# Attention: K and Q loaded in the row order of memory, by two transfers each

## The chip, the cores and the metric

The kernel runs on one core of a Trainium2 chip. The metric is the device time of one execution in microseconds, the median of the runs shown.

## The reference

The program is an attention with a compressive memory, followed by a layer of routed experts. For each of 8 x 8 heads, q, k and v have 576 rows of 64 float32 numbers:

```python
scores = (1/8) * q @ k.T, causal mask        # 576 x 576 per head
local  = softmax(scores) @ v
q_p    = where(q > 0, q, exp(q) - 1) + 1
mem    = (q_p @ M_prev) / (q_p @ z_prev + 1e-6)
x      = g * mem + (1 - g) * local           # g = sigmoid(beta), per head
# x as 4608 rows of 512; each row goes to one of 8 experts, 576 rows to each,
# in the order of the gate's logits; out = relu(x @ w1[e]) @ w2[e]
```

The change concerns the attention alone.

## The kernel before

**Units.** `attention` (line 290 on) works through 16 units `u` of 4 heads each: unit 2b holds heads 0 to 3 of batch b, unit 2b+1 heads 4 to 7. Several units are in work at once. A head's 576 rows are 4 blocks of 128 rows and a rest of 64.

**Layout.** `kf` and `qf` hold K and Q of a unit as 128 partitions x 18 blocks x 64 numbers. Blocks 4h to 4h+3 are the full blocks of head h. Blocks 16 and 17 hold the rests: heads 0 and 1 share block 16 (upper and lower 64 partitions), heads 2 and 3 share block 17. `load` (365) therefore needs for each of K and Q one transfer per head (373, 128 KB) and two for the rests (380, 32 KB each): six per unit. V has a similar layout, and a separate tile `vF` for head 3 of each unit (371, 372, 378).

**From K and Q to scores.** `turned` (443) splits the float32 numbers into two float16 halves in `h16` (the higher by ScalarE or GpSimd, the lower as a difference at line 457), turns the 18 blocks on TensorE (466) and copies them to `kT` and `qT`. SyncE copies 64 partitions of `kT` to `kB` (471) and of `qT` to `qM` (475); ScalarE or VectorE may do it instead. `maxes` (478) forms scores once to find the maximum of each row, with VectorE's reductions (480, 481). The 18 x 128 maxima are turned, read out into `mr` and sent by SyncE into a row of `qM` (540). `scores` (571) forms the scores a second time with the maxima subtracted, ScalarE takes the exponential, and `outs` (631) multiplies with V and with the memory. The result of a unit, `xs`, is written head by head; GpSimd does the last step of a head (`nsub`, 697).

**The end of a unit.** `fin` (699) has SyncE turn `xs` into `xT` by a DMA transpose (step `xt_`, 703) and write `xs` to memory (716, 717). TensorE multiplies `xT` by the gate's weights (step `lg`, 724).

**What sets the order.** Every step is an entry of one list `SC`, with the steps it depends on, the engine or engines that may do it, and the buffers that it takes and gives back. `PR_ORDER` (36) is a written list: the sequence of all 3118 step numbers, the chosen engine for each step with a choice, and the buffer for each step that takes one. `SC.run(PR_ORDER)` (766) issues the steps in that sequence, and each engine works through its own in order. SyncE does nothing but start transfers: all loads, `kB<-kT`, `qM<-qT`, the maxima, `xt_` and the writes of `xs` stand in its one queue. The expert part (`moe_all`) has its own plan.

**The first unit** is cut finer: `uo['0']` lists the pieces in which it is split, turned and copied, blocks 8 to 18 (heads 2 and 3 and the rests) first.

Of the kernel before, what the change touches and what calls it, by code (L numbers as in the profile page):

```python
# [33 lines left out]
 'uo': {'0': {'hord': [2, 3, 0, 1], 'ls': 1.0, 'mg': [[1], [0]], 'pc': [[8, 18], [0, 8]], 'pc_l': [[8, 18], [0, 8]], 'pc_p': [[8, 13], [13, 18], [0, 4], [4, 8]], 'pc_t': [[8, 18], [0, 8]], 'px': 2.0},  # L34
        'L': {'pet': 1}}}
PR_ORDER = ('''
# [253 lines left out]
def attention(ctx,tc,q,k,v,M_prev,z_prev,beta,wg,xd,L1,NB,cst,rcst):  # L290
# [60 lines left out]
    def K(t,i,a=0,b=18):  # L351

        return [(t,i,x) for x in range(a,min(b,16))]+([(t,i,16),(t,i,17)] if b==18 else [])
# [4 lines left out]
    def hord(u): return UO(u).get('hord') or [0,1,2,3]  # L358
# [3 lines left out]
    for u in range(NU):  # L362
        for h in FH(u): vfi[u,h]=len(vfi)
    def LS(u): return UO(u).get('ls',0.0)
    def load(u,nm,src,off,roff):
        b,hf=divmod(u,2); t={'k':kf,'q':qf,'v':vf}[nm][u%2]
        for j,h in enumerate(hord(u)):
            s=src[b,4*hf+h,off:off+512,:].rearrange('(t p) d -> p t d',p=128)
            if nm=='v' and h in FH(u):
# [66 lines left out]
    for u in range(NU):  # L436
# [125 lines left out]
        def vpieces(pc):  # L562
            return [(a,NVT if b_==18 else min(b_,NVT)) for a,b_ in pc]
# [7 lines left out]
        def scores(u=u,U2=U2,U3=U3):  # L571
# [25 lines left out]
            for j,h in enumerate(hord(u)):  # L597
                if len(gs)==2 and j%2==0: sj4(gs[j//2])
                B_=[]
                for w in range(3):  # L600
                    def f(x,h=h,w=w):
# [8 lines left out]
                        else:  # L610
                            two(p[:,0:256],4*h+2,qs(2)); mk(p[:,0:128])
                            for y in (2,0,1,3): two(p[:,256+64*y:320+64*y],4*h+y,lambda t: t[:,16+h2,64*hh:64*hh+64],last=True)
# [579 lines left out]
```

## Time and profile before

| | |
|---|---|
| median of 3 runs | 902.94 us (897.38 to 905.11) |
| profiled execution | 900.57 us, its span 898.5 us |
| TensorE (PE) busy | 809.4 us, 90% |
| VectorE (DVE), ScalarE (ACT), GpSimd (POOL) busy | 638.4, 584.2, 561.0 us |
| mean granted TensorE clock | 0.953 |
| DMA | 231675 packets, 120.58 MB |

Times in the rows are microseconds from the first instruction of the span, unless marked ns. L457 is line 457 of the kernel before. SPq is SyncE's queue of transfers; a row of it is the time that SyncE takes to start the transfer, not the transfer itself. The granted clock is a share of full speed: 1.0 is 2.4 GHz, 0.5 is 1.2 GHz. In a timeline, the bracket at the end says how long the engine had been idle before and what ended that. "x3" in a merged row is three instructions.

### The profile page before, as it was taken

Reading aid. Unit: us, or ns where it says so; the run is one execution under the profiler, and the core shown is the slowest. Engines: PE = TensorE matmul, PEld = TensorE weight load, DVE = VectorE, ACT = ScalarE, POOL = GpSimd, SP = SyncE. Lnnn points to the kernel's source line nnn. Section 1 sums busy time; section 2 is a strip of 40 time slices with the busy share of each in tenths; the row PEclk is TensorE's granted clock in tenths of the full one; section 3 lists DMA queues with packets and bytes.
Section 4 is the critical chain, followed back from the end, with each engine's and each line's share of the span. In section 5 each row is a group of like instructions: output and inputs, shape, how many; then the busy total and the mean of one; then the engine's idle time right before and its main releaser. Section 6 shows DMA issues by size and latency. Waiting matters only on the chain.

```text
span 898.5 us, 24664 instructions
## 1 busy us (share of the span) xinstructions
PE 809.4 (90%) x9432; PEld 539.1 (60%) x9432; DVE 638.4 (71%) x2276; ACT 584.2 (65%) x1062; POOL 561.0 (62%) x599
## 2 busy tenths in 40 slices
PE   4988989899999999997138999999999999999995
PEld 2767878787888888887016445454444444444442
DVE  8988969788898899887897778787868774111020
ACT  5988969686999889873337575757383845562110
POOL 4988869797899898885024383838183737852101
PEclk9999979899999999999557999999999999999998
DMA  5566687676666747433042565655564738920001
GB/s 126 128 139 148 156 168 147 158 156 134 147 148 158 171 99 163 99 73 84 1 140 102 187 141 211 139 215 130 204 141 142 200 127 190 279 109 18 36 12 42
DMA packets 231675, 120.58 MB, mean 134 GB/s; under 512 B 199493, under 2 KB 208709, under 8 KB 231557
## 3 DMA queue, kind: packets, MB, share of 16 engines
q1 hardware_dynamic: 225669, 100.13, 45.6%
q0 software_dynamic: 5888, 18.88, 6.8%
q8 instruction: 74, 1.21, 0.5%
q14 instruction: 44, 0.36, 0.1%
HBM read 72.40 MB, written 18.87 MB: 102 GB/s over the span
## 4 chain that ended last, share of the span: by engine, by line
PE 62%; issue 10%; DVE 10%; DMA 6%; POOL 5%; SPq 4%; ACT 2%; another core or an unknown queue 0%; POOLq 0%; DVEq 0%; ACTq 0%
PE py L834 16%; PE ph L834 15%; PE pb L306 13%; PE avo L306 9%; PE pb L466 3%; DVE scr L1075 2%; DMA qM<-qT 2%; PE prem L834 2%; SPq L373 2%; POOL h L457 2%; PE avm L306 1%; DMA xT<-xs 1%; PE pr L834 1%; DMA qf<-in_q_dram 1%; SPq L380 1%
## 5 line engine op out<-in xcount | busy, mean ns | idle before, releaser
L991 POOL TENSOR_TENSOR wl<-wst,wh 128x1024 f16<-128x1024 f32 x62 | 131.4, 2142 | 82.2 <-ACT wh L990 75.3
L834 PE MATMUL ph<-xT,wh 128*128 128x512 f16 (+1 forms) x560 | 164.8, 368 | 2.9 <-DVE hl L1034 1.4
L1053 POOL DMA_INDIRECT out_dram<-ys,idx x40 | 39.0, 975 | 118.7 <-ACT ys L1048 99.4
L834 PEld LDWEIGHTS <-wh 128*128 128x128 f16 x1072 | 69.2, 99 | 60.4 <-issue 4.7
L306 PE MATMUL pb<-qT,kT 128*128 128x64 f16 (+3 forms) x576 | 104.4, 243 | 1.0 <-ACT pf L627 1.0
L306 PE MATMUL pb<-qM,kB 128*128 128x64 f16 (+3 forms) x576 | 97.7, 242 | 5.7 <-DMA qM<-mr 3.8
L1034 DVE SCALAR_TENSOR_TENSOR hl<-ph,hh 128x512 f16<-128x512 f32 x64 | 44.0, 688 | 80.3 <-ACT hh L1033 77.5
L480 DVE TENSOR_REDUCE mx<-pb 128x1 f32<-128x512 f32 (+3 forms) x192 | 89.4, 503 | 14.6 <-PE pb L306 14.1
L834 PE MATMUL ph<-xT,wl 128*128 128x512 f16 (+1 forms) x280 | 98.4, 366 | 0.0
L834 PE MATMUL py<-wh,hh 128*128 128x512 f16 x256 | 97.0, 379 | 1.2 <-ACT hh L1033 0.8
L834 PE MATMUL py<-wl,hh 128*128 128x512 f16 x256 | 97.0, 379 | 0.0
L620 ACT ACTIVATE ph<-pb 128x512 f16<-128x512 f32 x144 | 85.2, 601 | 17.6 <-PE pb L306 11.4
L834 PE MATMUL prem<-xT,wh 128*128 128x64 f16 x512 | 96.6, 193 | 0.0
L1033 ACT ACTIVATE hh<-ph 128x512 f16<-128x512 f32 x64 | 38.0, 593 | 76.5 <-PE ph L834 55.4
L1075 DVE TENSOR_SCALAR_CACHE_REDUCE scr<-p_LwT,th 128x320 f16<-128x320 f32 x168 | 85.1, 543 | 2.9 <-DVE th L1082 0.2
L306 PE MATMUL pb<-kT,qM 128*128 128x512 f16 (+5 forms) x384 | 82.5, 312 | 5.1 <-DMA qM<-qT 2.4
L1073 ACT ACTIVATE scs<-p_LwT,th 128x320 f16<-128x320 f32 x84 | 47.0, 560 | 58.4 <-DVE th L1082 45.0
L834 PEld LDWEIGHTS <-hh 128*128 128x128 f16 x512 | 47.3, 97 | 55.8 <-ACT hh L1033 1.0
L306 PE MATMUL avo<-V,ph 128*128 128x65 f16 x1344 | 76.7, 193 | 0.0
L306 PE MATMUL avo<-V,pl 128*128 128x65 f16 x672 | 73.4, 196 | 1.3 <-POOL pl L628 1.3
L913 POOL DMA_INDIRECT xg<-xd,idx x40 | 38.9, 973 | 53.7 <-DVE sa L934 36.8
L306 PEld LDWEIGHTS <-ph 128*128 128x128 f16 x1344 | 69.2, 98 | 4.8 <-issue 1.5
(304 smaller groups left out, 2415.7 us busy)
## 6 DMA issues: line engine op xcount, KB each, us to landing
wst<-in_moe_w_dram SPq DMA_DIRECT2D x32, 1024.0 KB, 8.0
kf<-in_k_dram SPq DMA_DIRECT2D x64, 128.0 KB, 2.9
qf<-in_q_dram SPq DMA_DIRECT2D x64, 128.0 KB, 3.2
xd<-xs SPq DMA_DIRECT2D x16, 512.0 KB, 4.3
vf<-in_v_dram SPq DMA_DIRECT2D x48, 128.0 KB, 2.8
qM<-qT SPq DMA_DIRECT2D x15, 288.0 KB, 3.6
kB<-kT SPq DMA_DIRECT2D x14, 288.0 KB, 3.3
vF<-in_v_dram SPq DMA_DIRECT2D x16, 128.0 KB, 2.7
```

The costliest lines, as they stand in the source:

```text
L306: def MM(*a,**kw): mm(*a,skip_group_check=True,**kw)
L466: for i in range(a,b_): nc.tensor.transpose(p[:,128*(i-a):128*(i-a)+128],g()[:,i],cst['idh'])
L480: R=lambda o,i: nc.vector.tensor_reduce(o,i,axis=mybir.AxisListType.X,op=ALU.max)
L620: c=SC.add('Eh',[('A',486)],lambda x,a=a: nc.scalar.activation(phs_[x.buf['ph']][:,0:512],pbb[a.buf['pb']],AF.Exp,scale=0.125),acq=('ph',) ...
L834: def MM(*a,**kw): mm(*a,skip_group_check=True,**kw)
L913: SC.add('gather',[('P',1250 if i<4 else 1200,'p',0,(1250,'n'))],lambda x: G_.indirect_dma_start(out=xg[0:r_,i],out_offset=None,in_=xd,in_ ...
L991: SC.add('sp',[('P',2079)],lambda x,ws=ws,k=k,s=s: G_.tensor_sub(wl[:,k,s],ws(),wh[:,k,s]),r=[key+('h',)],w=[key+('l',)],after=[b],rel=rel ...
L1033: b=SC.add('hh',[('A',478)],lambda x,a0=a0,f=f: A_.activation(hh[:,f],phb[a0.buf['ph']],AF.Relu),w=[('hh',f)],after=[y],prio=pr('hh',n,pos ...
L1034: SC.add('hl',[('V',602)],lambda x,a0=a0,f=f: V_.scalar_tensor_tensor(hl[:,f],phb[a0.buf['ph']],0.0,hh[:,f],op0=ALU.max,op1=ALU.subtract), ...
L1053: SC.add('scat',[('P',1250 if i<4 else 1200,'p',0,(1250,'n'))],lambda x,e=e,i=i,r_=r_: G_.indirect_dma_start(out=outv[5*n+i],out_offset=ba ...
L1073: SC.add('sign',[('A',547)],lambda x,j=j,t_=t_,c_=c_: A_.activation(scs[j-KV],LwT,AF.Sign,bias=t_[:,4:5],accum_out=c_[:,j:j+1]),r=['LwT',( ...
L1075: V(462,lambda x,j=j,t_=t_,c_=c_: V_.tensor_scalar(scr[j],LwT,t_[:,j+1:j+2],0.0,op0=ALU.is_ge,op1=ALU.add,accum_out=c_[:,j:j+1]),r=['LwT', ...
```

## The change

K and Q of a unit are loaded as 2304 rows in the order of memory, 18 blocks of 128 rows: two transfers of 9 blocks each, four for each of K and Q in the first unit. Turned, the heads stand side by side: head h takes columns 576h to 576h+575 of `kT`, `qT`, `kB` and `pT` (the turned q_p). A head now begins and ends within a block, so the keys of dependence (`KC`, `KH`, `KR`) are counted by columns. `qM` keeps the old order, because the maxima's row does; the copy from `qT` becomes two, of 512 and of 64 columns of each head. V is loaded as before. The first unit is split at block 9 instead of 8. The number of steps falls from 3118 to 3013, and `PR_ORDER` is a new list throughout, with new choices of engine and buffer.

```diff
- 'uo': {'0': {'hord': [2, 3, 0, 1], 'ls': 1.0, 'mg': [[1], [0]], 'pc': [[8, 18], [0, 8]], ...
+ 'uo': {'0': {'hord': [2, 3, 0, 1],
...
+              'pc': [[9, 18], [0, 9]],
+              'pc_d': [[9, 13], [13, 18], [0, 4], [4, 9]],
...
 PR_ORDER = ('''
-5 21 2 23 26 4 22 25 0 24 1 28 27 3 32 31 41 30 43 42 29 45 6 44 47 248 ...
+5 21 2 22 24 1 23 26 4 25 3 27 28 37 6 39 240 0 41 38 241 43 42 34 40 44 ...
...
+    def KC(t,i,a,b): return K(t,i,a//128,(b+127)//128)
+    def KH(t,i,h): return KC(t,i,576*h,576*h+576)
+    def KR(t,i,h2): return KC(t,i,1152*h2+512,1152*h2+576)+KC(t,i,1152*h2+1088,1152*h2+1152)
...
     def load(u,nm,src,off,roff):
         b,hf=divmod(u,2); t={'k':kf,'q':qf,'v':vf}[nm][u%2]
+        if nm!='v':
+            rows=src[b,4*hf:4*hf+4].rearrange('h s d -> (h s) d')
+            for j,(a,b_) in enumerate(UO(u).get('pc_d') or [[0,9],[9,18]]):
+                SC.add('l'+nm,dq(182*(b_-a),hw=530),lambda x,a=a,b_=b_: nc.sync.dma_start(out=t[:,a:b_],in_=rows[128*a:128*b_].rearrange('(t p) d -> p t d',p=128)),w=K(nm+'f',u%2,a,b_),prio=pr('l'+nm,u,j*LS(u)))
+            return
...
-            SC.add('l'+nm,dq(182,hw=640),lambda x,hh=hh: nc.sync.dma_start(out=t[64*hh:64*hh+64,16:18,:],in_=r[hh,roff:roff+64,2*hf:2*hf+2,:]),w=[(nm+'f',u%2,16+hh)],prio=pr('l'+nm,u,1.5*LS(u)))
...
-        for a,b_ in MVP(u):
-            SC.add('qmove',... nc.sync.dma_start(out=qM[u%3][0:64,a:b_],in_=qTs[U3][64:128,a:b_]) ...
+        for h0,nh,kd in ([(0,4,0),(0,4,1)] if u else [(2,1,0),(3,1,0),(2,2,1),(0,1,0),(1,1,0),(0,2,1)]):
+            w_=512 if kd==0 else 64; o_=512*h0 if kd==0 else 2048+64*h0; n=nh*w_
+            def mv(x,h0=h0,nh=nh,kd=kd,w_=w_,o_=o_,n=n,U3=U3,u=u):
+                o=fl(qM[u%3])[0:64,o_:o_+n].rearrange('p (h k) -> p h k',k=w_); i=fl(qTs[U3])[64:128].rearrange('p (h k) -> p h k',k=576)[:,h0:h0+nh,512*kd:512*kd+w_]
+                if x.var=='d': nc.sync.dma_start(out=o,in_=i)
+                else: cp(x.var,o,i)
...
-            kq=lambda h,n: kT[:,4*h:4*h+n,:].rearrange('p a k -> p (a k)')
+            kq=lambda h,n: kT[:,576*h:576*h+128*n]
...
-            for c0_ in range(a,b_,8):
+            for c0_,c1_ in [(c,min(c+8,b_)) for c in range(a,b_,8)] if b_-a!=9 else [(a,a+4),(a+4,b_)]:
...
-            def two(o,jb,qsl,rows=None,last=False):
-                l=kT[:,jb] if rows is None else kT[:,jb,rows]
+            def two(o,h,jb,a,b,last=False):
+                l=slice(576*h+128*jb,576*h+min(128*jb+128,576)); qs=slice(576*h+a,576*h+b)
+                MM(o,kT[:,l],qT[:,qs],start=True,stop=False)
+                MM(o,kb_[:,l],qm_[:,512*h+a:512*h+b] if a<512 else qm_[:,2048+64*h:2112+64*h],start=False,stop=last)
...
-                        l=pT[:,4*h+i] if i<4 else pTf[:,128*(16+h2)+64*hh:128*(16+h2)+64*hh+128]
+                        l=pTf[:,576*h+128*i:576*h+128*i+128]
```

## Rows read from the trace of the kernel before

**Rows 1.** Windows by stage: length, busy us of PE, PEld, DVE, ACT, POOL, PEclk, DMA, GB/s.

```profile
0.00:22.00 22.00, 9.96 (x63) 6.12 (x64) 19.19 (x50) 12.91 (x21) 10.14 (x63) 1.00 0.56 126
22.00:73.00 51.00, 45.89 (x709) 37.08 (x706) 45.50 (x125) 45.65 (x87) 45.06 (x50) 1.00 0.59 133
73.00:221.00 148.00, 135.63 (x2285) 115.91 (x2282) 120.24 (x354) 117.39 (x223) 120.54 (x154) 0.93 0.74 156
221.00:395.00 174.00, 171.21 (x3036) 147.43 (x3034) 157.45 (x453) 155.12 (x292) 156.31 (x168) 1.00 0.58 130
...
424.00:898.50 474.50, 420.30 (x2831) 208.44 (x2829) 274.96 (x1233) 237.59 (x412) 210.20 (x143) 0.93 0.45 132
```

**Rows 2.** Waits of TensorE, 22 to 424 us: total us, times, longest.

```profile
PE pb L306 <- DMA xT<-xs: 6.6, 2, 3.6
PE pb L306 <- DMA qM<-mr: 3.8, 2, 2.1
PE pb L306 <- DMA qM<-qT: 2.4, 4, 1.0
PE pb L306 <- DMA qM<-zr: 1.9, 1, 1.9
```

**Rows 3.** Timeline of GpSimd and ScalarE: start, length, line, out<-in, idle before.

```profile
101.68 0.80 POOL L697 TENSOR_TENSOR xs<-xt,xs 128x320 f16<-128x320 f32 x1 [0.45 <-ACT xs L347]
...
204.09 0.25 ACT L347 CAST mr<-pb 18x128 f16<-18x128 f32 x1
```

**Rows 4.** Timeline of the transfers that SyncE starts (SPq).

```profile
102.43 2.83 SPq L373 DMA_DIRECT2D kf<-in_k_dram  x3
...
108.92 1.08 SPq L373 DMA_DIRECT2D qf<-in_q_dram  x2
...
110.63 3.80 SPq L703 DMA_TRANSPOSE xT<-xs  x1
...
210.04 0.84 SPq L540 DMA_DIRECT2D qM<-mr  x1
```

**Rows 5.** Timeline of TensorE, behind its two longest waits after the start.

```profile
117.29 0.70 PE L306 MATMUL pb<-wgs,xT 128*128 128x16 f16 x20 [3.59 <-DMA xT<-xs]
...
165.89 0.69 PE L306 MATMUL pb<-wgs,xT 128*128 128x16 f16 x20 [2.97 <-DMA xT<-xs]
```

**Rows 6.** Windows behind three waits of TensorE (clock third from the end).

```profile
115.00:130.00 15.00, 12.71 (x147) 11.23 (x148) 7.47 (x21) 7.02 (x13) 7.18 (x9) 0.66 0.77 169
165.00:175.00 10.00, 9.11 (x93) 7.42 (x94) 5.70 (x18) 5.82 (x13) 6.27 (x8) 0.66 0.74 186
210.00:220.00 10.00, 7.97 (x149) 7.37 (x149) 5.95 (x25) 5.36 (x10) 3.99 (x6) 0.83 0.94 166
```

**Rows 7.** Tiles kf, qf, qM: starts, ns min/median/max, first and last start.

```profile
L373 SPq DMA_DIRECT2D kf<-in_k_dram x64: 367/537/1807, 0.7 to 291.7; - x64
L380 SPq DMA_DIRECT2D kf<-in_k_dram x32: 596/628/1072, 1.8 to 293.5; - x32
...
L373 SPq DMA_DIRECT2D qf<-in_q_dram x64: 367/514/1828, 4.5 to 342.0; - x64
L380 SPq DMA_DIRECT2D qf<-in_q_dram x32: 595/623/1581, 5.6 to 334.0; - x32
...
L475 SPq DMA_DIRECT2D qM<-qT x15: 507/547/964, 29.6 to 361.7; - x15
```

**Rows 8.** Page, DMA issues: count, KB each, median us to landing.

```profile
kf<-in_k_dram SPq DMA_DIRECT2D x64, 128.0 KB, 2.9
...
qM<-qT SPq DMA_DIRECT2D x15, 288.0 KB, 3.6
```

**Rows 9.** Timeline of the start: SyncE's transfers, ScalarE.

```profile
0.74 1.01 SPq L373 DMA_DIRECT2D kf<-in_k_dram  x2
...
3.23 0.62 SPq L380 DMA_DIRECT2D kf<-in_k_dram  x1
...
6.47 1.28 ACT L347 ACT_TABLE_LOAD   x1 [6.47 <-DMA kf<-in_k_dram]
```

More of the change, by code (lines that the diff above doesn't have):

```diff
@@ L33 @@
  'strict': 1,
- 'uo': {'0': {'hord': [2, 3, 0, 1], 'ls': 1.0, 'mg': [[1], [0]], 'pc': [[8, 18], [0, 8]], 'pc_l': [[8, 18], [0, 8]], 'pc_p': [[8, 13], [13, 18], [0, 4], [4, 8]], 'pc_t': [[8, 18], [0, 8]], 'px': 2.0},
+ 'uo': {'0': {'hord': [2, 3, 0, 1],
+              'ls': 1.0,
+              'mg': [[1], [0]],
+              'pc': [[9, 18], [0, 9]],
+              'pc_d': [[9, 13], [13, 18], [0, 4], [4, 9]],
+              'pc_l': [[9, 18], [0, 9]],
+              'pc_p': [[9, 13], [13, 18], [0, 4], [4, 9]],
+              'pc_t': [[9, 18], [0, 9]],
+              'px': 2.0},
         'L': {'pet': 1}}}
 PR_ORDER = ('''
[75 rows of a table removed]
[72 rows of a table added]
 ''','''
[2 rows of a table removed]
[2 rows of a table added]
 ''','''
[6 rows of a table removed]
[6 rows of a table added]
 ''')
@@ L351, in K, with BK @@
     def K(t,i,a=0,b=18):
-        return [(t,i,x) for x in range(a,min(b,16))]+([(t,i,16),(t,i,17)] if b==18 else [])
+        return [(t,i,x) for x in range(a,b)]
+    def KC(t,i,a,b): return K(t,i,a//128,(b+127)//128)
+    def KH(t,i,h): return KC(t,i,576*h,576*h+576)
+    def KR(t,i,h2): return KC(t,i,1152*h2+512,1152*h2+576)+KC(t,i,1152*h2+1088,1152*h2+1152)
+    def BK(t,i,h,a,b=None): return KC(t,i,576*h+128*a,576*h+128*(a+1 if b is None else b))
     def KV_(t,i,a,b): return [(t,i,x) for x in range(a,b)]
@@ L375, in load @@
         for hh in range(2):
-            if nm=='v':
+            if 1:
                 g=[x for x in (0,1) if 2*x+hh not in FH(u)]
                 if g: SC.add('lv',dq(91*len(g),hw=640),lambda x,hh=hh,g=g: nc.sync.dma_start(out=t[64*hh:64*hh+64,RB+hh+2*g[0]:RB+hh+2*g[-1]+1:2,:],in_=r[hh,roff:roff+64,2*hf+g[0]:2*hf+g[-1]+1,:]),w=[('vf',u%2,RB+hh+2*x) for x in g],prio=pr('lv',u,1.5*LS(u)))
-                continue
-            SC.add('l'+nm,dq(182,hw=640),lambda x,hh=hh: nc.sync.dma_start(out=t[64*hh:64*hh+64,16:18,:],in_=r[hh,roff:roff+64,2*hf:2*hf+2,:]),w=[(nm+'f',u%2,16+hh)],prio=pr('l'+nm,u,1.5*LS(u)))
     def MK(u): return [(t,u%3,x) for t in ('qMm','qMr') for x in (0,1)]
@@ L462, in turned @@
                 for a,b_ in ch_:
-                    n=b_-a; px=(a<8)*PX(u)
+                    n=b_-a; px=(a<9)*PX(u)
                     def f(x,a=a,b_=b_):
@@ L471, in attention @@
             SC.add('kb',al('kb',u,d=819*(b_-a)/18+60,a=93+106*(b_-a),**(dict(v=69+33.3*(b_-a)) if u==0 else {})),lambda x,a=a,b_=b_,U2=U2,U3=U3: nc.sync.dma_start(out=kB[U2][0:64,a:b_],in_=kTs[U3][0:64,a:b_]) if x.var=='d' else cp(x.var,kB[U2][0:64,a:b_],kTs[U3][0:64,a:b_]),
-               r=K('kT',U3,a,b_),w=K('kB',U2,a,b_),prio=pr('kb',u,PX(u)*(a<8)))
+               r=K('kT',U3,a,b_),w=K('kB',U2,a,b_),prio=pr('kb',u,PX(u)*(a<9)))
         turned('q',qf,'qf',slice(64,128),qTs,'qT',U3)
-        for a,b_ in MVP(u):
-            SC.add('qmove',al('qmove',u,d=819*(b_-a)/18+60,a=93+106*(b_-a),**(dict(v=69+33.3*(b_-a)) if u==0 else {})),lambda x,a=a,b_=b_,U3=U3,u=u: nc.sync.dma_start(out=qM[u%3][0:64,a:b_],in_=qTs[U3][64:128,a:b_]) if x.var=='d' else cp(x.var,qM[u%3][0:64,a:b_],qTs[U3][64:128,a:b_]),r=K('qT',U3,a,b_),w=K('qM',u%3,a,b_),prio=pr('qmove',u,PX(u)*(a<8)))
+        for h0,nh,kd in ([(0,4,0),(0,4,1)] if u else [(2,1,0),(3,1,0),(2,2,1),(0,1,0),(1,1,0),(0,2,1)]):
[4 more added lines that the diff above has]
+                else: cp(x.var,o,i)
+            SC.add('qmove',al('qmove',u,d=.356*n+60,a=93+.833*n,**(dict(v=69+.26*n) if u==0 else {})),mv,r=[k_ for h in range(h0,h0+nh) for k_ in KC('qT',U3,576*h+512*kd,576*h+512*kd+w_)],w=[('qM',u%3,x) for x in (range(4*h0,4*h0+4*nh) if kd==0 else [16+x for x in range(2) if h0<=2*x<h0+nh])],prio=pr('qmove',u,PX(u)*(h0<2)+.1*kd))
         if u>2: SC.add('mz0',dq(26),lambda x,u=u: nc.sync.dma_start(out=qM[u%3][64:65],in_=qM[u%3][65:66]),r=[('qMz',u%3)],w=MK(u),prio=pr('MX',u,-40))
         def maxes(u=u,U2=U2,U3=U3):
-            kT,qT,mx=kTs[U3],qM[u%3],mxs[U2]
+            kT,qT,mx=fl(kTs[U3]),qM[u%3],mxs[U2]
             R=lambda o,i: nc.vector.tensor_reduce(o,i,axis=mybir.AxisListType.X,op=ALU.max)
@@ L493, in maxes @@
                 for j,h in enumerate(hs):
-                    kk=K('kT',U3,4*h,4*h+4)
+                    kk=KH('kT',U3,h)
                     def f(x,h=h):
@@ L503, in maxes @@
                     part('MX',f,f2,768,342,675,[('qM',u%3,4*h+2),('qM',u%3,4*h)]+kk,(h,1),x0+3*j+1)
-                kk=K('kT',U3,8*h2,8*h2+8)
+                kk=KH('kT',U3,2*h2)+KH('kT',U3,2*h2+1)
                 def f(x,h2=h2):
@@ L522, in g @@
                             o=misc[64*hh:64*hh+64,64*G.index(h2):64*G.index(h2)+64]
-                            MM(o,qT[:,16+h2,64*hh:64*hh+64],kT[:,16+h2,64*hh:64*hh+64],start=True,stop=False)
+                            MM(o,qT[:,16+h2,64*hh:64*hh+64],kT[:,576*(2*h2+hh)+512:576*(2*h2+hh)+576],start=True,stop=False)
                             MM(o,identb[:,0:64],maskM[:,0:64],start=False,stop=True)
-                rd=[('qM',u%3,16+x) for x in G]+[('kT',U3,16+x) for x in G]+rq
+                rd=[('qM',u%3,16+x) for x in G]+[k_ for x in G for k_ in KR('kT',U3,x)]+rq
                 a=SC.add('maxrem',[('T',75*n)],g,wg=256*n,r=rd,acq=('pb',),after=mf2.get(u-2,()),prio=pr('maxrem',u,jp))
@@ L550, in attention @@
             SC.add('phr',al('phr',u,a=Ac(n),**(dict(v=Vc(n)) if u==0 else {})),lambda x,a=a,b_=b_,U2=U2,UE=u%NE: (nc.scalar.activation(ef[UE][:,a:b_],qf[U2][:,a:b_],AF.Relu,scale=-1.0) if x.var=='a' else EV[x.var].tensor_scalar(ef[UE][:,a:b_],qf[U2][:,a:b_],-1.0,0.0,op0=ALU.mult,op1=ALU.max)),r=K('qf',U2,a,b_),w=K('ef',u%NE,a,b_),prio=pr('phr',u,PX(u)*(a==0)))
-            for c0_ in range(a,b_,8):
-                c1_=min(c0_+8,b_); n=n64(c0_,c1_); pv=lambda x,n=n: pbb[x.buf['pb']][:,0:n].rearrange('p (t d) -> p t d',d=64)
+            for c0_,c1_ in [(c,min(c+8,b_)) for c in range(a,b_,8)] if b_-a!=9 else [(a,a+4),(a+4,b_)]:
+                n=n64(c0_,c1_); pv=lambda x,n=n: pbb[x.buf['pb']][:,0:n].rearrange('p (t d) -> p t d',d=64)
                 y=SC.add('phe',[('A',75+.81*n)],lambda x,a=c0_,b_=c1_,UE=u%NE,pv=pv: nc.scalar.activation(pv(x),ef[UE][:,a:b_],AF.Exp,scale=-1.0),r=K('ef',u%NE,c0_,c1_),acq=('pb',),prio=pr('phe',u))
@@ L562, in vpieces @@
         def vpieces(pc):
-            return [(a,NVT if b_==18 else min(b_,NVT)) for a,b_ in pc]
+            e=lambda x: {9:8,18:NVT}.get(x,x)
+            return [(e(a),e(b_)) for a,b_ in pc]
         for a,b_ in vpieces(pieces(u,'vh')):
@@ L571, in scores @@
         def scores(u=u,U2=U2,U3=U3):
-            kT,qT,qm_=kTs[U3],qTs[U3],qM[u%3]
-            def two(o,jb,qsl,rows=None,last=False):
-                l=kT[:,jb] if rows is None else kT[:,jb,rows]
-                l2=kB[U2][:,jb] if rows is None else kB[U2][:,jb,rows]
-                MM(o,l,qsl(qT),start=True,stop=False)
-                MM(o,l2,qsl(qm_),start=False,stop=last)
+            kT,qT,qm_,kb_=fl(kTs[U3]),fl(qTs[U3]),fl(qM[u%3]),fl(kB[U2])
+            def two(o,h,jb,a,b,last=False):
+                l=slice(576*h+128*jb,576*h+min(128*jb+128,576)); qs=slice(576*h+a,576*h+b)
+                MM(o,kT[:,l],qT[:,qs],start=True,stop=False)
+                MM(o,kb_[:,l],qm_[:,512*h+a:512*h+b] if a<512 else qm_[:,2048+64*h:2112+64*h],start=False,stop=last)
             def sj4(G):
@@ L585, in g @@
                         o=misc[64*hh:64*hh+64,64*h2:64*h2+64]
-                        two(o,16+h2,lambda t: t[:,16+h2,64*hh:64*hh+64],slice(64*hh,64*hh+64))
+                        two(o,h,4,512,576)
                         MM(o,identb[:,0:64],maskT[:,0:64],start=False,stop=True)
-                rd=[('kBz',U2),('qMz',u%3)]+[(t,i,16+x_) for x_ in G for t,i in (('kT',U3),('kB',U2))]+[(t,u%3,x_) for t in ('qMm','qMr') for x_ in G]+[(t,i,16+x_) for x_ in G for t,i in (('qT',U3),('qM',u%3))]
+                rd=[('kBz',U2),('qMz',u%3)]+[(t,u%3,x_) for t in ('qMm','qMr') for x_ in G]+[k_ for x_ in G for t,i in (('kT',U3),('kB',U2),('qT',U3)) for k_ in KR(t,i,x_)]+[('qM',u%3,16+x_) for x_ in G]
                 c=slice(64*G[0],64*G[-1]+64); px=3*min(hord(u).index(h) for h in range(4) if h//2 in G)
@@ L602, in f @@
                         p=pbb[x.buf['pb']]; hh,h2=h%2,h//2
-                        qs=lambda a: (lambda t: t[:,4*h+a:4*h+4,:].rearrange('p a k -> p (a k)'))
                         mk=lambda o: MM(o,identb,maskT,start=False,stop=True)
                         if w==0:
-                            two(p,4*h,qs(0)); mk(p[:,0:128])
+                            two(p,h,0,0,512); mk(p[:,0:128])
                         elif w==1:
-                            two(p[:,0:384],4*h+1,qs(1)); mk(p[:,0:128])
-                            two(p[:,384:512],4*h+3,qs(3)); mk(p[:,384:512])
-                        else:
-                            two(p[:,0:256],4*h+2,qs(2)); mk(p[:,0:128])
-                            for y in (2,0,1,3): two(p[:,256+64*y:320+64*y],4*h+y,lambda t: t[:,16+h2,64*hh:64*hh+64],last=True)
+                            two(p[:,0:384],h,1,128,512); mk(p[:,0:128])
+                            two(p[:,384:512],h,3,384,512); mk(p[:,384:512])
+                        else:
+                            two(p[:,0:256],h,2,256,512); mk(p[:,0:128])
+                            for y in (2,0,1,3): two(p[:,256+64*y:320+64*y],h,y,512,576,last=True)
                     rd=[('qMm',u%3,h//2),('qMr',u%3,h//2),('kBz',U2),('qMz',u%3)]
-                    bk=[(4*h,),(4*h+1,4*h+3),(4*h,4*h+1,4*h+2,4*h+3)][w]; bq=[4*h+x for x in ((0,1,2,3),(1,2,3),(2,3))[w]]+([16+h//2] if w==2 else [])
-                    rd+=[(t,i,x_) for t,i in (('kT',U3),('kB',U2)) for x_ in bk]+[(t,i,x_) for t,i in (('qT',U3),('qM',u%3)) for x_ in bq]
+                    bk=[(0,1),(1,4),(0,4)][w]; bq=[(0,4),(1,4),(2,4.5)][w]
+                    rd+=[k_ for t,i,bb in (('kT',U3,bk),('kB',U2,bk),('qT',U3,bq)) for k_ in KC(t,i,576*h+128*bb[0],int(576*h+128*bb[1]))]+[('qM',u%3,4*h+x_) for x_ in range(bq[0],4)]+([('qM',u%3,16+h//2)] if w==2 else [])
                     a=SC.add('S',[('T',[492,553,511][w])],f,wg=[1152,1280,1152][w],r=rd,acq=('pb',),after=ch('S'),prio=pr('S',u,3*j+w)); res.append(a); ch('S',a)
@@ L661, in outs @@
             rv=[('V16g',U2)]+[(t_,U2,x) for x in list(range(4*h,4*h+4))+[RB+h] for t_ in ('V16h','V16l')]+['avz']
-            rm_=[('pT',U2,x) for x in list(range(4*h,4*h+4))+[16,17]]+[('mh',U2),('mh2',U2),('ml',U2),'avz']
+            rm_=KH('pT',U2,h)+[('mh',U2),('mh2',U2),('ml',U2),'avz']
             ce=[x for p in B_ for x in p]
```

163 rows, old and new, of the table PR_ORDER are left out of this document.

## The prediction

> **What bounds the kernel now.** I read the busy times by stage first [rows 1]. Their bounds follow the attention part, which ends near 424.5 us, and the expert part behind it, 474 us long, whose code and plan the change leaves alone. So everything has to come from the first 424.5 us. There TensorE is the busiest engine in each stage after the start, but not at one rate. From 221 to 395 us it runs 3036 matmuls in 174 us, 17.4 in a microsecond, at the full clock. From 73 to 221 us it runs 2285 in 148 us, 15.4 in a microsecond, at a mean granted clock of 0.93, and VectorE, ScalarE and GpSimd are less busy there (79 to 81%) than later (89 to 90%). So in the middle stage no other engine is full either. Something makes TensorE wait there that is not compute.
>
> The second view is what TensorE waited for [rows 2]. The two longest entries are the turned output (xT) and the copy of the row maxima (qM<-mr), both transfers that SyncE starts. Third, the timeline around the longest wait. The last head of that unit is written into xs by GpSimd at 101.68 + 0.80 = 102.48 us [rows 3], and the turning of xs starts only at 110.63 us [rows 4]. The reader is to see what fills those 8.1 us: SyncE starts eleven other transfers in a row without a gap, 0.5 to 1 us each, and seven of them are pieces of K and Q (the first row shows three of kf, the second two of qf, two more of qf stand between). TensorE gets to the logits, finds no xT, and stands for 3.59 us; the same happens at 165.89 us, 2.97 us idle [rows 5]. Before 212 us it stands 2.1 us for the maxima [rows 2]: ScalarE had them ready at 204.09 + 0.25 = 204.34 us [rows 3], and SyncE started their copy at 210.04 us [rows 4]. So SyncE's queue, which runs in order, is the hidden bound of the middle stage: not by bytes, but by the number of starts ahead of an urgent one.
>
> Each of the three waits costs twice. Behind them the granted clock falls to a mean of 0.66, 0.66 and 0.83 over 15, 10 and 10 us [rows 6], that is to the lower level, 1.2 GHz, for part of each stretch. The loss is at most 0.34 x 15 + 0.34 x 10 + 0.17 x 10 = 10.2 us. The waits themselves are 6.6 + 2.1 = 8.7 us. Together 18.9 us hang on three late starts.
>
> **The change part by part.** *Loads.* 64 + 32 starts for K and as many for Q go, 192 in all, with medians of 0.537, 0.628, 0.514 and 0.623 us [rows 7]: 34.4 + 20.1 + 32.9 + 19.9 = 107 us of SyncE's time. In come 4 + 4 for the first unit and 2 + 2 for each of the other fifteen, 68. A start of 288 KB is not in the trace. The rows do not grow with the bytes (32 KB takes longer to start than 128 KB), so the lower bound is 0.51 us; scaled by bytes it would be 2.25 x 0.54 = 1.2 us. I take 0.6, by the nearest rows: 41 us. The bytes and the 256-byte rows in memory stay the same, so the DMA engines' own work does not change. Net -66 us.
>
> *The copy of Q into qM.* One start becomes two (512 columns, then 64 for each head), because qM keeps its old order. By the written order nine of the fifteen second copies go by SyncE, 9 x 0.55 = 5 us [rows 7], and six by ScalarE. A ScalarE copy of 256 columns I bound by nothing and by twice its cast of 128 columns at 0.25 us [rows 3], so 3 us for six, laid beside the 10% or more that ScalarE has free [rows 1]; if that cover is gone it is 3 us. The first unit also sends three pieces of K by SyncE that ScalarE copied before: 2 us. The copy lands today in 3.6 us, 64 rows of 4.5 KB [rows 8]. Then it is 256 runs of 1 KB and 256 of 128 bytes. A load of 512 runs of 256 bytes lands in 2.9 us [rows 8], so 512 runs alone do not make it slow. I take no change for the sum, and keep up to double (another 3.6 us) for the range.
>
> *Net on SyncE:* about -59 us of starts, nearly all between 0 and 342 us, where the last Q load is started [rows 7]. *Everything else:* the number of transposes, score matmuls and reductions is the same; heads side by side only move column offsets. The first unit's split at 9 instead of 8 blocks adds one ScalarE exp and one VectorE operation of some 0.5 us each, inside the start.
>
> *The start.* ScalarE can first work on K at 6.47 us, because the first half of K needs four transfers and the last of them is the fifth that SyncE starts, at 3.23 us [rows 9]. With the change that half needs the first two starts, and the second of two begins halfway through the first row, near 1.25 us, so it lands some 2.0 us sooner. But VectorE is busy 19.2 of the first 22 us [rows 1], so the gain lies between 0 and 2.4 us. I take 1.5.
>
> *22 to 73 us.* Here VectorE, ScalarE and GpSimd are each busy 88 to 90%, so they are next in line. One TensorE wait of 1.9 us for the first unit's maxima (qM<-zr) is again SyncE's [rows 2]. I take 2 us, between 0 and 5 (its idle time).
>
> *73 to 221 us.* Of the seven K and Q starts ahead of the first late turning about 68/192 of them, 2 or 3, remain: 4.5 x 0.65 = 2.9 us of its 3.59 us, before counting that SyncE arrives less late. At the maxima before 210 us three of the starts in 5.7 us are K's. The new order helps too. Counted in the two written orders, from the last nsub step of a unit to its xt_ step, there stand 79 SyncE steps over units 0 to 14 before and 34 after; from the reading of the maxima to their copy, 15 and 4. Bounds: 0, if other transfers fill the queue again, and 18.9 us, if all three waits and their clock go. A check of the upper end: 2285 matmuls at the later stage's 17.4 take 131 us, 17 less. Then GpSimd and VectorE are late next, as in the later stage, where they are 90% busy and TensorE still loses only 2.8 of 174 us. I take 11.5, some 60%, because a wait that only shrinks may still cost the clock.
>
> **The sum:** 1.5 + 2 + 11.5 = 15 us. The profiled execution took 900.57 us, so it becomes 885.6. It lies 2.4 us under the median of the runs, 902.94; against that median, 888.
>
> **The rivals.** *No gain: it is not the starts.* The Trainium skill, "DMA: Bandwidth & Descriptors", section "Issuing engines are not separate DMA queues", says that the time a sequencer takes to initiate a DMA is usually small relative to the DMA itself. By that rule SyncE's queue could not be what is late, and removing starts that keep all bytes would give back only the start of the kernel. In rows: the DMA engines are busy 0.74 of the middle stage [rows 1]; if their rings hold the turning back, it lands as late as now, and its place in the queue does not matter. That leaves 1.5 us: 901. To this belongs that GpSimd or VectorE gives back what SyncE frees. Against it: a start is 0.54 us [rows 7] against a landing of 2.9 us [rows 8], but the starts follow each other while the transfers overlap, and the 8.1 us between the last head and the turning were spent before it was even started [rows 3, 4]. Chance 0.22, times 894 to 908.
>
> *Slower: the copy of Q.* The maxima of a unit wait for it, and TensorE already waited for it four times [rows 2]. If the copy in short runs lands in 7.2 instead of 3.6 us, four such waits grow by 3.6 us, and at the ratio of the three stalls above (10.2 us of clock for 8.7 us of wait) cost 4 x 3.6 x 2.2 = 31 us, 16 more than the forecast gains: 919. It decides from a landing of about 5.3 us on, where 4 x 1.7 x 2.2 = 15. For it: the same skill page, in its "Specifications", sets 512 bytes as the least transfer for line rate, and the second copy has runs of 128. Against it: the 512 runs of 256 bytes above, and that the other eleven copies found TensorE with other work. Chance 0.12, times 912 to 920.
>
> *The order undoes it.* All attention steps are in a newly written order, so a new late step can appear where none was. By TensorE's steps it is near the old one: each unit's maxima, scores and logits come in almost the same sequence as before. I count this within the two rivals above.
>
> **Numbers.** What a measurement of this kernel can tell from no change is 1%: 893.9 to 912.0 us. The forecast has 0.66, at 876 to 894 us; no gain 0.22; slower 0.12. Range 876 to 905: the lower end is 24 under the profiled run (18.9 of the middle stage, 2.4 of the start, 5 of the second stage, less 2), the upper takes in most of the second case and leaves out the third. Faster 0.66, same 0.22, slower 0.12.
>
> **What would show it.** In the profile of the changed kernel: kf and qf with 34 starts each near 0.6 us; the idle of TensorE behind xT<-xs and qM<-mr under 3 us in all; the granted clock at 1.0 from 73 to 221 us, or one short dip; the attention part ending near 409 us; ScalarE's wait for the first K ending near 4.5 us. It is wrong if starts of 288 KB take over 1 us, if qM<-qT lands later than 5 us and heads the waits, or if the turnings start at once and TensorE stands all the same.

## The result, and the profile after

The changed kernel takes 873.31 us (median of 4 runs, 872.08 to 873.77). The kernel before took 902.25 us beside it (median of 4 runs). The ratio is 0.9683, interval 0.9639 to 0.9727: 28.9 us gained where I had forecast 15. The profiled execution is the one of 872.08 us, with a span of 870.2 us against 898.5.

The attention part gave nearly all of it. The last multiplication with the gate's weights, which closes the attention, starts 26.6 us sooner. The first fence is TensorE's timeline of the kernel before, the second that of the changed kernel (start, length, line, out<-in).

```profile
423.89 0.58 PE L306 MATMUL pb<-wgs,xT 128*128 128x8 f16 x17 [0.54 <-DVE xT L348]
```

```profile
397.26 0.61 PE L311 MATMUL pb<-wgs,xT 128*128 128x8 f16 x17 [0.53 <-DVE xT L353]
```

The windows by stage of the changed kernel, with the columns of [rows 1]:

```profile
0.00:22.00 22.00, 10.73 (x69) 6.61 (x70) 18.91 (x53) 14.11 (x26) 12.14 (x67) 1.00 0.75 156
22.00:73.00 51.00, 48.90 (x780) 39.85 (x780) 48.47 (x132) 50.04 (x96) 49.58 (x56) 1.00 0.81 172
73.00:221.00 148.00, 146.20 (x2623) 125.73 (x2623) 137.85 (x410) 135.44 (x256) 136.81 (x169) 1.00 0.80 165
221.00:395.00 174.00, 171.55 (x3117) 149.75 (x3117) 154.71 (x451) 143.55 (x275) 152.64 (x169) 1.00 0.58 124
395.00:424.50 29.50, 4.71 (x46) 3.01 (x46) 22.96 (x124) 7.87 (x24) 1.87 (x3) 0.52 0.06 21
```

The row to look at is the third. From 73 to 221 us TensorE now runs 2623 matmuls, 17.7 in a microsecond, where it ran 2285 [rows 1]. It is busy 146.2 of 148 us at a granted clock of 1.00 throughout, and VectorE, ScalarE and GpSimd are busy 92 to 93%. The middle stage now runs at the pace of the later one (17.9 matmuls in a microsecond).

What TensorE waited for, 16 to 420 us, in the changed kernel (total, times, longest):

```profile
PE pb L311 <- DMA qM<-qT: 1.6, 2, 1.2
PE pb L311 <- DMA vf<-in_v_dram: 0.9, 1, 0.9
...
PE pb L311 <- DMA qM<-mr: 0.2, 1, 0.2
```

The waits for xT, 6.6 us in [rows 2], are gone altogether; those for the maxima fell from 3.8 to 0.2 us. SyncE's queue shows why. The changed kernel's timeline around one turning, first GpSimd's last write of a head, then SyncE's starts, then TensorE's use:

```profile
95.44 0.78 POOL L713 TENSOR_TENSOR xs<-xt,xs 128x320 f16<-128x320 f32 x1
...
96.08 1.62 SPq L379 DMA_DIRECT2D qf<-in_q_dram  x1
97.79 0.58 SPq L732 DMA_DIRECT2D xd<-xs  x1
98.42 0.58 SPq L494 DMA_DIRECT2D qM<-qM  x1
99.06 3.15 SPq L719 DMA_TRANSPOSE xT<-xs  x1
...
107.55 0.64 PE L311 MATMUL pb<-wgs,xT 128*128 128x16 f16 x20
```

The head is written at 96.22 us and the turning starts at 99.06, 2.8 us later instead of 8.1, with three starts ahead of it instead of eleven. TensorE comes to the logits with no idle time in front of them.

The loads themselves, by tile (starts, ns min/median/max, first and last start), and from the page's DMA issues (count, KB each, median us to landing), of the changed kernel:

```profile
L379 SPq DMA_DIRECT2D kf<-in_k_dram x34: 377/566/1187, 0.7 to 278.4; - x34
...
L379 SPq DMA_DIRECT2D qf<-in_q_dram x34: 368/535/1690, 2.9 to 316.8; - x34
...
qf<-in_q_dram SPq DMA_DIRECT2D x30, 288.0 KB, 4.4
kf<-in_k_dram SPq DMA_DIRECT2D x30, 288.0 KB, 4.0
...
qM<-qT SPq DMA_DIRECT2D x15, 256.0 KB, 3.2
```

A start of 288 KB takes 0.54 to 0.57 us, like one of 128 KB [rows 7]. The larger loads land later (4.0 to 4.4 us against 2.9 [rows 8]), and TensorE does not stand for them at any time from 16 to 420 us.

### The profile page after: what moved, and what is told of

Its sections match the earlier page's. It is cut to its first block, busy times and chain, and to the rows that moved or that the text cites. A ratio compares the mean times of both kernels' runs of the same rounds, so it can differ in the third digit from the quotient of the medians.

```text
span 870.2 us, 24506 instructions
## 1 busy us (share of the span) xinstructions
PE 796.7 (92%) x9432; PEld 530.4 (61%) x9432; DVE 636.2 (73%) x2278; ACT 580.7 (67%) x1062; POOL 561.9 (65%) x603
## 4 chain that ended last, share of the span: by engine, by line
PE 69%; issue 10%; DVE 9%; POOL 5%; DMA 3%; ACT 2%; SPq 1%; another core or an unknown queue 1%; POOLq 0%; DVEq 0%; ACTq 0%
PE py L850 16%; PE pb L311 16%; PE ph L850 15%; PE avo L311 12%; PE pb L478 4%; DVE scr L1091 3%; PE prem L850 2%; PE avm L311 2%; PE pr L850 1%; DMA qM<-qT 1%; POOL out_dram L1069 1%; POOL h L469 1%; DMA vf<-in_v_dram 1%; PE pl L850 1%; DMA wst<-in_moe_w_dram 1%
## 5 line engine op out<-in xcount | busy, mean ns | idle before, releaser
L311 PE MATMUL pb<-qT,kT 128*128 128x64 f16 (+3 forms) x576 | 102.2, 242 | 0.3 <-DVE ef L571 0.2
L497 DVE TENSOR_REDUCE mx<-pb 128x1 f32<-128x384 f32 (+3 forms) x192 | 89.9, 504 | 7.0 <-PE pb L311 6.0
L311 PE MATMUL pb<-kT,qM 128*128 128x512 f16 (+5 forms) x384 | 79.9, 307 | 4.7 <-DMA qM<-qT 1.6
```

What stands on the lines that cost most here:

```text
L311: def MM(*a,**kw): mm(*a,skip_group_check=True,**kw)
L497: R=lambda o,i: nc.vector.tensor_reduce(o,i,axis=mybir.AxisListType.X,op=ALU.max)
```

## The experiments

Two theories. **A:** the number of starts in SyncE's queue held the attention back, and the gain is the starts taken out. **B:** the gain is something else that came with the change: the newly written order, or the larger transfers. Three more questions follow from A: which starts, what a late one costs, and in which stage. All ratios are against the kernel before on the same chip in the same session. Microseconds are not compared across sessions: the expert part, which no kernel here changes, took 467 to 474 us in the profiled executions. Where two kernels are set side by side, I therefore also give the time at which the attention ends (the end of the last multiplication with the gate's weights): 424.5 us before, 397.9 in the changed kernel. Each of these times is of one profiled execution.

**Six starts again, in the new order.** Each 9-block load of units 1 to 15 becomes three of 3 blocks (ST = 3); order, layout and bytes stay. The first unit's loads, of 4 and 5 blocks, become two each as well, so 128 starts come back and not the 120 of the expectation.

```diff
-lambda x,a=a,b_=b_: nc.sync.dma_start(out=t[:,a:b_], ...)
+lambda x,a=a,b_=b_: [nc.sync.dma_start(out=t[:,c:min(c+ST,b_)], ...) for c in range(a,b_,ST)]
```

> The changed kernel with its layout and its written order, but each load of 9 blocks of K and Q (units 1 to 15) started as three transfers of 3 blocks: six starts per tensor and unit again, same bytes, same 256-byte rows. Theory 1 (the number of starts in SyncE's queue): 120 starts of about 0.54 us come back, 65 us of SyncE's time, and the time goes back to 893 to 905 us, with the waits for xT and qM<-mr back and the clock falling behind them. Theory 2 (the newly written order does it, whatever the number of starts): it stays at 872 to 878 us. In between, both have a part, in that proportion.

Measured: 1.0031 (1.0009 to 1.0054). The whole gain is gone; the attention ends at 426.3 us. Two windows of this kernel, and TensorE's waits from 22 to 390 us:

```profile
22.00:73.00 51.00, 39.48 (x565) 31.38 (x563) 37.57 (x98) 38.98 (x73) 38.16 (x39) 0.93 0.60 135
73.00:221.00 148.00, 137.01 (x2363) 115.95 (x2362) 126.28 (x372) 123.37 (x232) 122.76 (x158) 0.97 0.73 153
...
PE pb L312 <- DMA qM<-qT: 13.7, 10, 3.5
PE pb L312 <- DMA qM<-mrx: 4.4, 1, 4.4
PE pb L312 <- DMA qM<-mr: 4.0, 2, 3.0
```

The late transfer is now mostly the copy of Q, not the turning: which one is late differs between the two orders, but with six starts some transfer is late in both. From 22 to 73 us 565 matmuls run instead of 780. The DMA engines are less busy than in the changed kernel (0.60 and 0.73 against 0.81 and 0.80), and the copy of Q lands 3.3 us after its start, against 3.2. So it is late because it starts late, and not because transfers are slower.

**Small starts beside the large ones.** The changed kernel, with two starts of 2 KB behind each K and Q load of units 1 to 15: the number of starts is that of before, the bytes nearly those of after.

```diff
-lambda x,...: nc.sync.dma_start(out=t[:,a:b_], ...)
+lambda x,...: (nc.sync.dma_start(out=t[:,a:b_], ...), more(u))   # two starts of dm<-k, 2 KB each
```

> The changed kernel with its loads whole, and behind each load of K and Q of units 1 to 15 two more starts of 2 KB into a tile that nobody reads: as many starts as with six per tensor, at the same places, but K and Q still land as two transfers. Theory 1 (SyncE's time for a start is what counts): as with three transfers of 3 blocks, 0.99 to 1.01 of the kernel before. Rival (it is K and Q in pieces, which land later, or the DMA engines): 0.97 of the kernel before, as the changed kernel.

Measured: 0.9991 (0.9968 to 1.0014). The 120 starts, by tile, and the waits, of this kernel:

```profile
L377 SPq DMA_DIRECT2D dm<-in_k_dram x120: 420/593/1961, 6.2 to 347.6; - x120
...
PE pb L311 <- DMA qM<-qT: 14.9, 9, 3.3
PE pb L311 <- DMA qM<-mr: 2.9, 2, 1.6
```

0.24 MB of transfers that nobody waits for undo 28 us; the copy of Q again lands in 3.3 us. It is the starts in SyncE's queue, not the data or the size of a transfer.

**The old order with two starts, late and early.** In the kernel before, each of K and Q of units 1 to 15 is loaded by two row-order transfers: once both at the last of the old six steps, once at the first old steps where the buffer is free.

```diff
+            if len(seen)==6: [nc.sync.dma_start(out=t[:,a:a+9], ...) for a in (0,9)]      # late
...
+            a=9*(len(seen)-1-AT[nm][u])                                                   # early
+            if a in (0,9): nc.sync.dma_start(out=t[:,a:a+9], ...)
```

> The kernel before with its written order and layout of the work, but K and Q of units 1 to 15 loaded by two transfers of 9 blocks in the order of memory, both at the place of the last of the six old steps. The rows then stand in the wrong blocks, which the rest of the kernel does not know: the output is not the reference's, only the time counts. Theory 1 (number of starts): 120 starts fewer, SyncE is no longer late, 873 to 885 us. Theory 2 (the order): 895 to 905 us, as before. In between, both have a part.

Measured: 0.9917 (0.9898 to 0.9935). Most of the gain is missing. This kernel's middle stage, TensorE's waits from 22 to 221 us, and one wait of GpSimd:

```profile
73.00:221.00 148.00, 137.87 (x2313) 117.30 (x2310) 123.50 (x365) 119.80 (x227) 125.88 (x158) 0.94 0.80 165
...
PE avo L306 <- POOL pl L634: 4.8, 1, 4.8
PE pb L306 <- DMA qM<-qT: 3.2, 2, 1.6
PE pb L306 <- DMA xT<-xs: 2.7, 1, 2.7
...
POOL h L349 <- DMA qf<-in_q_dram: 6.0, 1, 6.0
```

GpSimd stands 6 us for Q and TensorE then for GpSimd: that load came too late. That pointed at the place, not the number, so the early variant was run.

> As the kernel before with K and Q of units 1 to 15 in two transfers, but each pair is started at the first of the old six steps at which the buffer is free, not at the last (the rows again stand in the wrong blocks, only the time counts). Theory A (the old order gained only 0.8% because its loads came too late): 0.97 to 0.98 of the kernel before. Theory B (the old order was laid out for late starts, and has other waits that only a new order removes): 0.985 to 0.995, with waits for xT and the clock dips still there.

Measured: 0.9697 (0.9663 to 0.9731), the same as the changed kernel within the intervals; the attention ends at 399.1 us. The windows of this kernel:

```profile
22.00:73.00 51.00, 48.84 (x779) 39.83 (x777) 48.93 (x134) 50.07 (x99) 49.65 (x57) 1.00 0.77 153
73.00:221.00 148.00, 147.59 (x2638) 126.70 (x2636) 138.54 (x412) 135.80 (x257) 138.15 (x172) 1.00 0.80 167
```

With the old sequence of steps and the old copy of Q, fewer starts, placed early, give the whole gain. The new order adds nothing that can be told from the spread of the runs. Theory B falls in both its forms.

**Are three late starts enough?** The kernel before, with 34 loads moved from ahead of its three late starts to behind them; number of starts unchanged.

```diff
...
+    for s_,ls_ in BEHIND:
+        for i in ls_: ids.remove(str(i))
+        p_=ids.index(str(s_))+1; ids[p_:p_]=map(str,ls_)
```

> The kernel before with all its starts, but 34 loads of K, Q and V that stand ahead of the three late starts (the turnings of units 1 and 3, the copy of unit 7's maxima) moved directly behind them in the written order; their first readers stand 98 steps or more later. Theory 3 (the forecast's: the loss hangs on these three late starts and the clock behind them): the three waits and the clock dips go, 18.9 us less at most, 883 to 890 us. Theory 1 (SyncE is late everywhere, and the three waits are only where it shows): the lateness comes out elsewhere, 893 to 902 us.

Measured: 1.0144 (1.0102 to 1.0186), slower, and outside both expectations. The waits of this kernel, and the longest of them with the start that it hangs on:

```profile
PE pb L307 <- DMA qM<-mr: 9.8, 3, 7.6
PE pb L307 <- DMA qM<-qT: 5.8, 4, 2.3
PE pb L307 <- DMA xT<-xs: 4.3, 1, 4.3
...
166.96 0.85 SPq L541 DMA_DIRECT2D qM<-mr  x1
...
169.02 0.21 PE L307 MATMUL pb<-qM,kB 128*64 128x64 f16 x1 [7.64 <-DMA qM<-mr]
```

The same starts made other transfers late, by more. Ahead of this copy of the maxima stand thirteen loads (157.89 to 166.86 us), twelve of them put there by the edit. So moving starts moved the wait: the three waits of [rows 2] are not a loss that belongs to these three places. Whether some better order of the same starts would do is not shown by this one.

**What a late start costs.** The changed kernel, with eight starts of 2 KB ahead of the turnings of units 1 and 3.

```diff
+def ahead(u):
+    if u in LATE: [nc.sync.dma_start(out=dm[:,8*(u//2)+j],in_=k[0,j,0:128,0:4]) for j in range(8)]
...
-lambda x: nc.sync.dma_start_transpose(out=xTs[x.buf['xT']],in_=fl(xs()))
+lambda x: (ahead(u), nc.sync.dma_start_transpose(...))
```

> The changed kernel with eight small starts (2 KB each, into a tile that nobody reads) ahead of the turning of units 1 and 3. Each turning starts 8 x 0.6 = 4.8 us later; the logits of these units come 2 to 2.5 us after their xT lands in the changed kernel. If a late start costs its wait and the clock behind it: two waits of 2 to 3 us and as much again by the clock, 4 to 10 us more, 877 to 884 us. If TensorE's time is set by something else: no change, 872 to 875 us.

Measured: 0.9829 (0.9799 to 0.9859), some 13 us above the changed kernel's 0.9683. In the profile its attention ends 10.2 us later. The rows of this kernel:

```profile
73.00:221.00 148.00, 142.62 (x2413) 121.50 (x2412) 129.04 (x382) 126.64 (x240) 127.06 (x161) 0.95 0.76 152
...
152.00:167.00 15.00, 14.03 (x119) 11.66 (x120) 6.97 (x24) 7.15 (x16) 8.66 (x14) 0.54 0.67 154
...
PE pb L312 <- DMA xT<-xs: 3.5, 2, 2.0
```

Two waits, 3.5 us in all, came back, and with the second, which ends at 152.97 us, the granted clock falls to a mean of 0.54 over 15 us: a loss of at most 0.46 x 15 = 6.9 us. Elsewhere in the stage it stays at 1.00. Together 10.4, near the 10.2 measured. A microsecond of waiting cost three.

**Half the starts, and one.** ST = 5 makes four starts for each of K and Q; one transfer of 18 blocks at the place of the second step makes one. The latter writes the first half of the buffer at a step that is ordered for the second half alone, so its output is not the reference's and only its time counts.

```diff
+ST = 5
...
+(u and not a) or nc.sync.dma_start(out=t[:,0 if u else a:b_], ...)
```

> The changed kernel with each load of 9 blocks started as two (5 and 4 blocks), four starts per tensor and unit: 60 more than the changed kernel, 60 fewer than with three pieces. If the time goes with SyncE's load, half of the way, 0.98 to 0.99 of the kernel before. If there is a threshold (the queue is late only once it is full), near 0.97 or near 1.00.

> The changed kernel with one transfer of 18 blocks per tensor for units 1 to 15, started at the place of the second of the two: 30 starts fewer again. If SyncE still sets the time, 0.5 to 1% under the changed kernel, 0.96 of the kernel before. If the queue has room now and TensorE is the bound, no change, 0.965 to 0.972; if the later place of the first half makes K and Q late, slower, 0.975 to 0.985.

Measured: 0.9734 (0.9705 to 0.9763) with four, 0.9778 (0.9748 to 0.9808) with one. The interval with four overlaps that of the changed kernel, 0.9639 to 0.9727; the attention ends at 404.3 us, 6.5 later. The windows with four:

```profile
22.00:73.00 51.00, 45.76 (x722) 37.24 (x722) 45.39 (x122) 47.55 (x92) 47.16 (x53) 1.00 0.73 160
73.00:221.00 148.00, 144.20 (x2566) 123.54 (x2563) 136.37 (x403) 133.04 (x253) 133.50 (x166) 1.00 0.80 161
```

So the first sixty starts put back cost 6.5 us, and the next 68, up to six for each of K and Q, 22.0. The clock is part of that: with four it is not lowered in either stage, with six it is 0.93 and 0.97, at most 0.07 x 51 + 0.03 x 148 = 8 us. One start is worse than two (the attention ends at 403.9 us): it waits for the whole buffer (SyncE stands 5.5 us behind GpSimd's reading of K and Q, 1.2 in the changed kernel), and the copy of Q is late five times (4.5 us in all). The optimum lies at two among the variants tried.

**In which stage?** Six starts in units 1 to 5 alone, and in units 6 to 15 alone.

```diff
+N = lambda u: 3 if 0<u and u<6 else 9      # the other kernel: u>5
+... for c in range(a,b_,N(u))]
```

> The changed kernel with six starts for each of K and Q in units 1 to 5 alone (40 starts more, nearly all before about 90 us); units 6 to 15 keep two. Theory A, the queue is full where its starts would take longer than the work between them: with the six starts everywhere the stretch from 22 to 73 us ran 565 matmuls instead of 780, which at 15.3 in a microsecond is 14 us; that loss comes back here and stays, and from 90 us on everything runs as in the changed kernel (17.7 matmuls in a microsecond): ratio to the kernel before near 0.984 (0.980 to 0.988). Theory B, lateness in the second stage is made up later and the gain sits in the middle stage, where the prediction put it: at most 5 us lost, ratio 0.974 or less.

> The same with six starts for each of K and Q in units 6 to 15 alone (80 starts more, nearly all after about 80 us). Theory A: 22 to 73 us as in the changed kernel (near 780 matmuls), the other half of the loss comes back in 73 to 300 us with waits for qM and xT and a lower granted clock: ratio near 0.986 (0.980 to 0.992). Theory B: nearly the whole gain goes, ratio 0.995 or more.

Measured: 0.9831 (0.9799 to 0.9863) early, 0.9794 (0.9765 to 0.9824) later, the second just under what theory A expected. The windows of the two kernels, early first:

```profile
22.00:73.00 51.00, 42.91 (x633) 34.10 (x631) 40.66 (x109) 41.98 (x81) 41.37 (x43) 0.97 0.59 133
73.00:221.00 148.00, 142.76 (x2521) 122.06 (x2521) 135.09 (x399) 133.21 (x251) 133.31 (x170) 1.00 0.77 166
```

```profile
22.00:73.00 51.00, 49.26 (x781) 39.81 (x779) 48.52 (x133) 49.94 (x96) 49.34 (x54) 1.00 0.80 171
73.00:221.00 148.00, 141.14 (x2436) 120.36 (x2435) 130.48 (x386) 127.69 (x242) 128.13 (x162) 0.98 0.72 154
```

Each part takes back a third to a half: what is lost early is not made up later. The two losses, 1.5 and 1.1 points, add up to 2.6 of the 3.5 that six starts everywhere cost; by the end of the attention (410.8 and 411.3 us) they are 12.9 and 13.4 of 28.4 us. The kernel with six everywhere has the first unit's eight starts besides.

**The queue's own account.** I added up the durations of SyncE's starts, cut at the ends of each stretch. The first number is their share of the stretch; beside it is the number of matmuls that TensorE ran. Even between two starts that follow at once lie 0.04 to 0.1 us, which are not in the share.

| kernel | 22 to 73 us | 73 to 221 us | attention ends, us | ratio |
|---|---|---|---|---|
| before | 0.88, 709 | 0.89, 2285 | 424.5 | 1 |
| loads behind | 0.87, 730 | 0.84, 2236 | 431.8 | 1.014 |
| six starts | 0.90, 565 | 0.85, 2363 | 426.3 | 1.003 |
| small starts | 0.91, 576 | 0.88, 2334 | 428.0 | 0.999 |
| old order, two late | 0.68, 729 | 0.81, 2313 | 418.5 | 0.992 |
| six, early units | 0.90, 633 | 0.74, 2521 | 410.8 | 0.983 |
| late turning | 0.84, 781 | 0.74, 2413 | 408.1 | 0.983 |
| six, later units | 0.89, 781 | 0.83, 2436 | 411.3 | 0.979 |
| one start | 0.90, 765 | 0.74, 2539 | 403.9 | 0.978 |
| four starts | 0.90, 722 | 0.80, 2566 | 404.3 | 0.973 |
| old order, two early | 0.76, 779 | 0.80, 2638 | 399.1 | 0.970 |
| changed | 0.87, 780 | 0.72, 2623 | 397.9 | 0.968 |

The share never passes 0.91; with the short pauses (up to 0.15 us) counted in, the kernel before stands at 0.96 and 0.97, the changed one at 0.94 and 0.77. At TensorE's pace of 2623 matmuls in the middle stage the starts of the kernel before would need 0.97 x 2623/2285 = 1.11 of the time (1.02 without the pauses): more than there is. So SyncE was not merely in the way of three transfers; by this estimate it bounded that stage. That fits the price of a start: up to four starts 24.5 us more of SyncE's time moved the end of the attention by 6.5 us, from four to six 34.5 us moved it by 22.0, the lower clock included.

The share alone doesn't decide everything. From 22 to 73 us the kernel before and the changed one stand at 0.88 and 0.87 and run 709 and 780 matmuls. The late turnings and the old order with late loads lose with a queue that has room in the middle stage, at 0.74 and 0.81. So the place of the starts counts too. A turning holds SyncE longest, for 3.1 to 5.0 us, as long as some six loads, and the six from 73 to 221 us take 24.0 us in the kernel before, where the K and Q loads take 47.2. The 3.33 us wait of the kernel with small starts, for one, is for a copy of Q that stood behind a turning:

```profile
142.78 4.70 SPq L723 DMA_TRANSPOSE xT<-xs  x1
...
148.21 0.63 SPq L494 DMA_DIRECT2D qM<-qT  x1
...
152.87 0.50 PE L311 MATMUL pb<-kT,qM 128*128 128x384 f16 x1 [3.33 <-DMA qM<-qT]
```

The table shows what goes together; that starts are the cause rests on the kernels that change nothing else.

## Why the prediction was too small

The direction, the engine and the queue as the cause were right; the range missed the time because of one term. The table sets side by side the times at which the same number of matmuls had started, at the ends of [rows 1]'s stages:

| stage of before | predicted | measured |
|---|---|---|
| start to 22 us | 1.5 | 1.1 |
| 22 to 73 us | 2, between 0 and 5 | 3.5 |
| 73 to 221 us | 11.5, between 0 and 18.9 | 19.6 |
| after 221 us | 0 | 2.4 in the attention, 1.7 in the expert part |

**The failed step** is "I take 11.5, some 60%, because a wait that only shrinks may still cost the clock". It measured 19.6. None of the three waits was left to shrink: all went, and with them the whole clock loss, 0.93 to 1.00. So did the shorter waits, which the upper bound left out: TensorE's idle time in the stage fell from 12.4 us [rows 1] to 1.8, and the three waits were 8.7 of it. I had counted which starts stood ahead of one turning, and kept 2 or 3 of seven. What the runs point to is the sum over the stage: 0.89 of it in starts before, 0.72 after. That "18.9 us hang on three late starts" was too narrow as well: with the same starts moved, the time was lost at other transfers. My own check of the upper end, 2285 matmuls at the later stage's 17.4 in a microsecond, gave 17 us and was the better estimate. It only needed the question whether the queue still had reason to be late.

**22 to 73 us** came out above the 2 us for the same reason: TensorE's idle time there fell from 5.1 us [rows 1] to 2.1 us, while VectorE, ScalarE and GpSimd rose from 88 to 90% to 95 to 98%. I had taken them as next in line at 90%; they had room.

**The range** reached down to 876 with some terms at their bounds and 2 us taken off for none. With all at their bounds (2.4 + 5 + 18.9 under 900.57) it would have reached 874.3, still above the profiled 872.08. The three stages gained 24.2 of these 26.3 us; the 4.1 us after 221, which I set at nothing, are what carried the time past the bound. SyncE's loads go on until 342 us [rows 7], and I closed the account at 221. The 1.7 us of the expert part are within the 467 to 474 us that this part took from run to run, so they need not belong to the change.

**The start** was right in size: ScalarE's wait for the first K ended near 4.0 us (forecast 4.5, before 6.47 [rows 9]), and 1.1 us of it reached TensorE.

**Loads:** 0.566 and 0.535 us for a start of 288 KB (forecast 0.6), so not by bytes. **The copy of Q** lands in 3.2 us instead of 3.6 [rows 8] in spite of its short runs; ScalarE's copy of 256 columns took 0.40 us (bounded by 0 and 0.5). The slower rival is refuted.

**The rival "it is not the starts"** is refuted by the small starts, 0.9991. The Trainium skill, "DMA: Bandwidth & Descriptors", section "Issuing engines are not separate DMA queues", calls the sequencer's time to initiate a DMA usually small relative to the DMA. Here that holds for one transfer (0.55 us against 4.0 to 4.4), but not for a queue of them: in the kernel before, the starts alone take 0.89 of the middle stage.

**"The new order helps too"** is not supported: the old order with two early starts does as well. The 79 against 34 SyncE steps that I counted in the two written orders need no second cause.

What stays open: why the old order with late loads lost where it did. The waits name late loads; a variant between late and early was not run.

## What to carry to other kernels

Add up the start times in each in-order queue stage by stage, not only ahead of the transfer that is visibly late. A queue near 0.9 busy beside a TensorE that runs below its own pace elsewhere is a suspect, even if each start is half a microsecond and every engine shows free time; a few small starts more, of data that nobody reads, are a cheap test of it. If a change takes such a queue well below that, estimate the stage at the pace of an unhindered one (here 17.4 matmuls in a microsecond, which gave 17 of the 19.6 us), clock included, and do not discount it wait by wait. Merging transfers pays only as long as the merged one can still start early: two transfers beat four and one here, and the same two started late lost most of the gain.

## What was not expected of the hardware

The time to start a transfer did not follow its bytes: medians of 0.593 us for 2 KB, 0.537 for 128 KB [rows 7] and 0.566 for 288 KB. A copy between two tiles in runs of 1 KB (256 KB, 3.2 us) and of 128 bytes (32 KB, 2.8 us) landed no later than one in rows of 4.5 KB (288 KB, 3.6 us [rows 8]). And two waits of at most 2.0 us each took up to 6.9 us of granted clock on top of their own 3.5.
